# An H3 convolution block with an MLP on one core: SyncE's transfers wait for the landing of the sixth ahead in place of the fourth

## The chip, the cores and the metric

The kernel runs on one core of a Trainium2 chip. The core has a matrix engine (TensorE, PE in the profile; its weight loads are PEld), a vector engine (VectorE, DVE), a scalar engine (ScalarE, ACT), a general engine (GpSimd, POOL) and a fifth one, SyncE (SP), which here does nothing but issue transfers between the chip's memory (HBM) and the core's own buffer (SBUF). Sixteen DMA engines carry these transfers. The metric is the device time of one execution in microseconds. Three executions of the kernel before took 695.85, 694.62 and 696.65 us; their median, 695.85 us, is the time before.

## The reference

With S = 2048 positions, D = 640 channels and F = 1728 hidden features, all in float32:

```python
x = A_q
mod = (_silu(c) @ w_mod).reshape(c.shape[0], 6, 1, -1)
sa, ca, ga, sb, cb, gb = (mod[:, 0], mod[:, 1], mod[:, 2], mod[:, 3], mod[:, 4], mod[:, 5])
h = _layernorm(x, axis=-1) * (1 + ca) + sa
x = x + ga * _A_ref(h, A_k, A_v, A_shift_k, A_ssm_k, A_ssm_D)
h = _layernorm(x, axis=-1) * (1 + cb) + sb
x = x + gb * _B_ref(h, B_w1, B_b1, B_w2, B_b2)
return x
```

`_A_ref(q, k, v, ...)` convolves k with 4 taps per channel, multiplies by v (the product is called kv), convolves kv along the whole sequence with a kernel of 2048 taps per channel (written as an FFT of length 4096, a product and the inverse), adds `kv * ssm_D`, and multiplies by q. `_B_ref` is a matmul with w1, a bias, a squared relu, a matmul with w2 and a bias.

## The kernel before, in words

**The two halves.** The first half, up to some 290 us, is the convolution block. It runs over five blocks b of 128 channels. The long convolution is an FFT built of matmuls: `unit_a` (L383, the first factor: small matmuls of 64 columns, tile `pa`), `spectrum` (L398, tiles `x`, `h` and `eh`), a product on DVE and POOL, `back` (L464, tile `qp`), `unit_t` (transposes, L530) and `unit_y` (L541, tile `y`). `unit_a` for block b + 1 is spread over the second part of block b. The second half is the MLP: eight chunks of 256 positions by fourteen blocks of 128 hidden features, with `mlp_front` (L720, tile `h`) and `mlp_back` (L790, tile `acc`). Its weights and the intermediate result x1 come in by DMA.

**The transfers.** Nearly every transfer is issued by SyncE through one helper, `sp_dma` (L138). In the first half these are, block by block: k and v for the short convolution (tile `KV`, 256 KB each); the kernel ssm_k, in four parts (tile `p`, rows of 256 bytes); kv, stored to a scratch tensor `kv_d` and loaded back transposed in four parts (also into `p`); q whole (`q`, for the layernorm's statistics) and by channel block (`xp`); tables (`gb`, `gi`); slices of w_mod (`wm`, 320 KB each), from which the rows of the modulation are summed on ACT and POOL and taken up by PE (`mr`); and stores of x1 (`x_d`). SyncE runs its instructions in order, so a transfer that waits holds back all that are written behind it. ACT issues eight small transfers and POOL two, on queues of their own.

**What sets the order.** The order of the work in the first half is written out by hand in a table: `at(GS(1, 5), ...)` puts calls at a numbered place between the units of block 1. At the end of the program `keep_order` ties each engine's instructions to the order in which they were written. A transfer's place in SyncE's order is therefore fixed. Three things can hold it there: its data or its buffer (semaphores of PE, DVE, ACT, POOL), the landing of an earlier transfer on which it depends, and the rule in `sp_dma`: once more than `OUT` transfers have been issued, each waits for the landing of the one that stands `OUT` places ahead of it:

```python
def sp_dma(o, i):
    sp.dma_start(o, i)
    queued.append(nc.cur_bb.bb.instructions[-1].name)
    if len(queued) > OUT:
        info = mybir.DependencyInfo(mybir.DependencyClass.Sync, mybir.DependencyReason.DATA)
        tc.add_manual_dep(nc.cur_bb.bb.instructions[-1], queued[-1 - OUT], info, reason="place in time")
```

With `OUT = 4` (L29) no more than four of SyncE's transfers are under way at a time. Landings are told through eight semaphores, which SyncE's and ACT's transfers use in turn.

Of the kernel before, what the change touches and what calls it, by code (L numbers as in the profile page):

```python
# [25 lines left out]
NC = S // CH  # L26
EPS = 1e-5
MLAG = 3
OUT = 4  # L29


def _constants():
# [60 lines left out]
def ssm_mlp_kernel(  # L93
# [43 lines left out]
# [7 lines that stand above are left out]
# [1135 lines left out]
```

## Time and profile before

| what | us |
|---|---|
| median of three executions | 695.85 |
| the profiled execution's own time | 693.38 |
| its span, first to last instruction | 691.6 |
| PE busy in the span | 657.0 |
| DVE, ACT, POOL busy | 335.9, 330.1, 311.4 |

The granted TensorE clock of the profiled execution was 0.997 on the mean. SyncE issued 243 transfers; the core's DMA engines moved 74.76 MB, at 108 GB/s over the span.

How to read it: "busy" is time in which an engine executes; waiting, branching and the issue of transfers do not count. The page cuts the span into 40 slices and gives a digit for each, in tenths of full. A row such as "A L1 <- B x L2: 6.1, 6, 2.0" in the view of waits says that engine A, at line 1, was idle for 6.1 us in total, 6 times and 2.0 us at the longest, until B at line 2 released it; "issue" in place of B means that nothing which the profile shows released it. The chain of waits follows the work that ended last back to the start, each piece with its start and its duration. In the view of windows each engine has its busy time and, in brackets, its number of instructions; behind these stand the granted clock, the share of the sixteen DMA engines and GB/s. Rows of DMA queues give packets, megabytes and the share of the stretch; q1 is SyncE's queue, and queues of the kind "instruction" carry the engines' instructions. Rows of DMA issues give the count, the size of each and the median time from issue to landing.

### The profile page before, as it was taken

To read this page: it belongs to the slowest core of one execution; us is meant where nothing else is said; L and a number is where in the kernel's file an instruction comes from. 1 tells how busy PE (TensorE), PEld (TensorE's weight loads), DVE (VectorE), ACT (ScalarE), POOL (GpSimd) and SP (SyncE) were. 2 spreads that over 40 slices of the span, in tenths; PEclk is the share of its full clock that TensorE was granted. 3 is DMA by queue.
4 is the path that set the end of the run, shared out by engine and by line. 5 is a ranking of instruction groups with operands and counts; after the bars stand their busy time and mean duration, and the time that the engine had idled before them with its cause. 6 is when DMAs were issued, how large, how long until landed. Compare 5 with 4: busy or idle time off the path is not lost.

```text
span 691.6 us, 21100 instructions
## 1 busy us (share of the span) xinstructions
PE 657.0 (95%) x9164; PEld 630.8 (91%) x9164; DVE 335.9 (49%) x601; ACT 330.1 (48%) x688; POOL 311.4 (45%) x390
## 2 busy tenths in 40 slices
PE   6699898889999999999999999999999999999996
PEld 4689798778898888889999999999999999999996
DVE  5267584658886697487532322323332332422313
ACT  4436656767976976466324333333233233233221
POOL 1062165359869789443523514415325325225213
PEclk9999999999999999999999999999999999999999
DMA  9897998889671643466020010100200200200101
GB/s 234 244 270 230 233 265 233 236 204 233 191 221 34 173 148 113 127 199 181 1 77 1 26 52 1 41 37 1 77 1 1 77 1 1 77 1 1 39 1 39
DMA packets 110960, 74.76 MB, mean 108 GB/s; under 512 B 48658, under 2 KB 96146, under 8 KB 110868
## 3 DMA queue, kind: packets, MB, share of 16 engines
q1 hardware_dynamic: 108912, 72.87, 37.2%
q8 instruction: 72, 1.18, 0.7%
q10 hardware_dynamic: 1892, 0.54, 0.4%
q14 instruction: 20, 0.16, 0.1%
q0 software_dynamic: 64, 0.01, 0.0%
HBM read 58.98 MB, written 14.42 MB: 106 GB/s over the span
## 4 chain that ended last, share of the span: by engine, by line
PE 81%; DVE 6%; ACT 5%; DMA 4%; issue 2%; POOL 1%; DVEq 0%; POOLq 0%; ACTq 0%; SPq 0%
PE acc L790 27%; PE h L720 26%; PE qp L464 5%; PE pa L383 4%; PE x L398 4%; PE y L541 4%; PE h L398 3%; DMA wm<-in_w_mod_dram 3%; PE t L530 2%; PE h L711 1%; PE xtp L685 1%; DVE KV L261 1%; ACT wx L146 1%; DVE kacc L261 1%; PE vt L276 1%
## 5 line engine op out<-in xcount | busy, mean ns | idle before, releaser
L151 POOL TENSOR_TENSOR mtmp<-mtmp 128x256 f32<-128x256 f32 x112 | 71.4, 638 | 244.4 <-ACT mtmp L752 236.5
L720 PE MATMUL h<-xt,w_S 128*128 128x256 f32 x1290 | 167.5, 281 | 1.1 <-DVE w_S L157 1.1
L720 PEld LDWEIGHTS h<-xt,w_S 128*128 128x128 f32 x1290 | 161.7, 190 | 1.3 <-DVE w_S L157 1.3
L790 PE MATMUL acc<-w_S,hring 128*128 128x320 f32 x960 | 156.6, 311 | 0.2 <-DVE hring L157 0.2
L157 DVE TENSOR_TENSOR hring<-mtmp,hring 128x256 fp32r<-128x256 f32 x112 | 65.4, 584 | 168.3 <-ACT hring L146 168.3
L790 PEld LDWEIGHTS acc<-w_S,hring 128*128 128x128 f32 x960 | 141.7, 188 | 0.8 <-DVE hring L157 0.7
L752 ACT ACTIVATE mtmp<-h,b1t 128x256 f32<-128x256 f32 x104 | 49.4, 475 | 174.0 <-PE h L720 170.8
L146 ACT ACTIVATE hring<-mtmp 128x256 fp32r<-128x256 f32 x112 | 46.5, 416 | 48.8 <-POOL mtmp L151 47.5
L383 PE MATMUL pa<-wx,p 64*64 64x64 f32 x2560 | 49.3, 228 | 10.8 <-issue 6.1
L383 PEld LDWEIGHTS pa<-wx,p 64*64 64x64 f32 x2560 | 43.9, 141 | 16.8 <-issue 11.3
L146 ACT ACTIVATE a<-pa 128x512 f32<-128x512 f32 x80 | 43.5, 608 | 19.7 <-PE pa L383 19.2
L151 DVE TENSOR_TENSOR wx<-x,wx 128x512 f32<-128x512 f32 x64 | 40.8, 683 | 18.9 <-PE x L398 7.7
L541 PE MATMUL y<-wx,wx 128*64 128x64 f32 x1280 | 43.9, 224 | 2.9 <-ACT wx L146 1.6
L541 PEld LDWEIGHTS y<-wx,wx 128*64 128x64 f32 x1280 | 39.9, 138 | 7.4 <-issue 3.4
L398 PE MATMUL x<-a,gb 128*64 128x128 f32 x640 | 41.6, 274 | 3.3 <-DVE wx L151 2.1
L687 DVE TENSOR_SCALAR we<-xtp,cbs 128x256 f32<-128x256 f32 x35 | 19.0, 543 | 46.8 <-PE xtp L685 46.8
L398 PEld LDWEIGHTS x<-a,gb 128*64 128x64 f32 x640 | 35.9, 137 | 4.9 <-PE h L398 3.0
L154 POOL TENSOR_TENSOR wm<-wm,wm 128x640 f32<-128x640 f32 x20 | 32.1, 1606 | 16.9 <-ACT wm L341 16.5
L261 DVE SCALAR_TENSOR_TENSOR KV<-kt,tap,KV 128x511 f32<-128x511 f32 (+2 forms) x48 | 35.9, 748 | 7.6 <-ACT ktail L146 6.0
L146 ACT ACTIVATE q<-qp 128x512 f32<-128x512 f32 (+1 forms) x40 | 21.3, 584 | 35.4 <-PE qp L464 35.4
L398 PE MATMUL h<-a,gb 128*64 128x128 f32 x512 | 34.0, 275 | 1.5 <-ACT wx L146 1.5
L790 PE MATMUL acc<-w_WX,hring 128*128 128x320 f32 x192 | 31.4, 312 | 0.0
(142 smaller groups left out, 1014.2 us busy)
## 6 DMA issues: line engine op xcount, KB each, us to landing
wm<-in_w_mod_dram SPq DMA_DIRECT2D x25, 320.0 KB, 4.1
KV<-in_A_k_dram SPq DMA_DIRECT2D x20, 256.0 KB, 4.6
KV<-in_A_v_dram SPq DMA_DIRECT2D x20, 256.0 KB, 4.4
p<-in_A_ssm_k_dram SPq DMA_DIRECT2D x20, 256.0 KB, 4.7
p<-kv_d SPq DMA_DIRECT2D x20, 256.0 KB, 4.1
xp<-in_A_q_dram SPq DMA_DIRECT2D x20, 256.0 KB, 4.3
q<-in_A_q_dram SPq DMA_DIRECT2D x15, 320.0 KB, 4.5
out_dram<-x SPq DMA_DIRECT2D x14, 320.0 KB, 2.2
```

Source lines behind the costliest of these rows:

```text
L146: act.activation(o, i, AF.Copy)
L151: eng.tensor_mul(o, a, b)
L154: eng.tensor_add(o, a, b)
L157: eng.tensor_sub(o, a, b)
L261: dve.scalar_tensor_tensor(o, tk[:, : 512 - t], tap[:, b, t : t + 1], o, op0=ALU.mult, op1=ALU.add)
L383: pe.matmul(t[e][64 * r : 64 * r + 64, g].rearrange("p m d -> p (m d)"), pt[b][l, i, 8 * q + g, :], cw[l, r], start=True, stop=True,)
L398: pe.matmul(t[64 * a : 64 * a + 64, s + r], gb[:, g, r, a], AX[b][i][:, 2 * g + a], start=True, stop=True,)
L464: pe.matmul(t[a][:, u], gi[l, 4 * j + u, r], w[r][l, u % 2], start=(r == 0), stop=(r == 1),)
L541: pe.matmul(y[64 * h : 64 * h + 64, 4 * (g % 2) + i].rearrange("p c l d -> p (c l d)"), tss[g][:, i, 64 * r : 64 * r + 64], ca[:, r, h], s ...
L720: pe.matmul(hps[n, f][:m], WI[1, f][:, a, b], XT[n][:, x, b], start=(b == 0 and i == 0), stop=(b == NB - 1 and i == 2),)
L752: act.activation(r[:m], h[:m], AF.Relu, bias=b1t[:m, f : f + 1])
L790: pe.matmul(acc[2 * s + i], h[:, a, s * P : (s + 1) * P], w[:, y, i * 320 : (i + 1) * 320], start=(f == 0 and ti == 0), stop=(f == NF - 1 ...
```

## The change

The constant `OUT` goes from 4 to 6. Each of SyncE's transfers, from the seventh on, then waits for the landing of the sixth ahead of it, and no more than six are under way. Nothing else differs: the instructions on PE, DVE, ACT and POOL are the same in the same order, and SyncE's transfers too; on SyncE only the semaphores that are waited for differ.

```diff
 NC = S // CH
 EPS = 1e-5
 MLAG = 3
-OUT = 4
+OUT = 6
```

## The prediction

> **What bounds the kernel now.** I read the page first, then the windows by stage, what PE and SP wait for, the chain of waits, and last the DMA queues of single stretches.
>
> ```profile
> span 691.6 us, 21100 instructions
> PE 657.0 (95%) x9164; PEld 630.8 (91%) x9164; DVE 335.9 (49%) x601; ACT 330.1 (48%) x688; POOL 311.4 (45%) x390
> DMA  9897998889671643466020010100200200200101
> ...
> q8 instruction: 72, 1.18, 0.7%
> ```
>
> PE is idle for 691.6 - 657.0 = 34.6 us. The DMA engines are nearly full for the first third and almost empty after it. The windows say where the idle time lies:
>
> ```profile
> core 0: us, PE busy (x) PEld busy (x) DVE busy (x) ACT busy (x) POOL busy (x), PEclk, DMA share, GB/s
> 60.00:90.00 30.00, 26.58 (x765) 24.24 (x758) 20.53 (x43) 18.84 (x36) 5.69 (x17) 1.00 0.91 252
> ...
> 120.00:150.00 30.00, 25.26 (x632) 22.30 (x634) 18.68 (x40) 19.58 (x36) 11.89 (x16) 1.00 0.75 213
> ...
> 205.00:240.00 35.00, 33.28 (x894) 30.20 (x892) 22.08 (x32) 27.99 (x58) 28.45 (x27) 1.00 0.34 95
> ...
> 320.00:680.00 360.00, 360.00 (x2756) 360.00 (x2755) 116.73 (x234) 120.87 (x270) 128.06 (x160) 1.00 0.08 28
> ```
>
> From 320 us on PE never stops, so nothing done to transfers can move that half: whatever the change is worth is decided before. There PE loses 3.4 us (60 to 90) and 4.7 us (120 to 150) where the DMA engines are full, and 1.7 us of 35 where they are a third full, with more matmuls in it (894). What PE waits for, longest first:
>
> ```profile
> PE pa L383 <- issue: 6.1, 6, 2.0
> PE kt L239 <- DMA KV<-in_A_k_dram: 4.3, 1, 4.3
> PE pa L383 <- DMA p<-kv_d: 3.1, 2, 2.3
> ```
>
> The largest row is "issue": no semaphore holds PE. And on the chain of waits:
>
> ```profile
> 21.47 3.14 DMA kv_d<-kacc
> ...
> 27.71 5.22 PE pa L383 x214
> 32.93 1.58 issue
> 34.51 0.83 PE pa L383 x39
> ...
> 79.50 0.61 issue
> ...
> 82.99 1.36 issue
> ...
> 114.65 0.40 issue
> ...
> 120.35 4.30 DMA wm<-in_w_mod_dram
> ...
> 124.73 6.76 DMA wm<-in_w_mod_dram
> ...
> 140.88 7.30 DMA wm<-in_w_mod_dram
> ```
>
> Four of these issue stalls (1.58, 0.61, 1.36, 0.40 us) are on it, all in the middle of a run of the 64-column pa matmuls. My reading is that PE's next instructions have not arrived. Queue q8 carries 72 packets, and PE has 2 x 9164 = 18,328 matmuls and weight loads: one packet for each 255, so a fetch for each 127 matmuls. A pa run takes 5.22 us for 214, some 3.1 us for 127: faster than anywhere else. The DMA queues of the stretch 31.9 to 32.4 us have one such packet, just before PE stops at 32.93; those of 310 to 680 us have 23, and PE waits for none of them:
>
> ```profile
> q8 instruction: 1, 0.02, 13.9%
> ```
> ```profile
> q8 instruction: 23, 0.38, 0.4%
> ```
>
> So a fetch that meets full DMA engines is late, and one that meets empty ones is not.
>
> **The change, part by part.** No instruction is added or moved; the order on all five engines is the same. Only SP's waits change: transfer n waits for the landing of n-6, not n-4. Waits for data stay. What SP waits for in 0 to 175 us (first and last of the thirteen DMA rows over 0.1 us, and the largest other row):
>
> ```profile
> SPq L138 <- DMA wm<-in_w_mod_dram: 12.6, 11, 3.8
> ...
> SPq L138 <- PE mr L323: 3.6, 3, 2.1
> ...
> SPq L138 <- DMA tap<-in_A_shift_k_dram: 0.2, 1, 0.2
> ```
>
> The thirteen rows sum to 80.9 us, all others to some 18: for 82% of SP's waiting the change lets it go on, until it stands six deep or meets a wait for data.
>
> *Do transfers land sooner?* Time to landing, in this full stretch and where a transfer is nearly alone:
>
> ```profile
> q1 hardware_dynamic: 69112, 40.82, 86.8%
> ...
> KV<-in_A_k_dram SPq DMA_DIRECT2D x18, 256.0 KB, 4.6
> ```
> ```profile
> out_dram<-x SPq DMA_DIRECT2D x14, 320.0 KB, 2.2
> ```
> ```profile
> x_d<-xp SPq DMA_DIRECT2D x15, 256.0 KB, 2.6
> ```
>
> With three ahead it is 4.6 us, alone 2.2 to 2.6: each transfer ahead costs about (4.6 - 2.4) / 3 = 0.7 us. The 40.82 MB in 175 us on q1 are 233 GB/s, about what four transfers of 256 KB in 4.6 us make (228). Four lone transfers in 2.4 us would be 437 GB/s, so the path is full, not the count of four. With six I expect 4.6 + 2 x 0.7 = 6.0 us to landing at the same rate, and transfers that land when they did. Two places on the chain can gain. The store at 21.47 took 3.14 us, alone 2.6: with the gb loads ahead of it issued earlier, 0 to 0.5; I take 0.3. The wm transfer at 124.73 goes out as that of 120.35 lands (124.65), the fourth ahead of it; SP was ready after its issue at 123.36 (0.46 us), so 0 to 0.8; it stands in the same line, so I take 0.4. Gain: 0.7 us.
>
> ```profile
> 123.36 0.46 SPq L138 DMA_DIRECT2D kv_d<-KV  x1
> ```
>
> *What is later?* Everything that shares the DMA engines and isn't SP's own, and that is the fetches. If a fetch waits for what stands in the engines ahead of it, two more transfers delay it by 2 x 0.7 = 1.4 us, and as PE is already standing when it comes, the stall grows by as much. If it doesn't wait for them, 0. The row of 310 to 680 us, with no stall, against 6.1 us of them in the full part is nearer to the first. At 34.51 and 115.05 four p loads went out just before:
>
> ```profile
> 24.68 2.92 SPq L138 DMA_DIRECT2D p<-kv_d  x4
> ...
> 115.30 4.74 SPq L138 DMA_DIRECT2D p<-kv_d  x4
> ```
>
> Their issue held SP for 2.92 and 4.74 us (the issue above took 0.46), so there SP gets perhaps one further ahead, 0.7 us. The four stalls on the chain then cost 2 x 1.4 + 2 x 0.7 = 4.2 us; times the 82%, 3.4. A fifth adds nothing, as the chain runs over the wm loads beside it:
>
> ```profile
> 131.39 0.45 PE L383 MATMUL pa<-wx,p 64*64 64x64 f32 x13 [2.01 <-issue]
> ```
>
> Fetches that now come just in time may start to stall; how near they are no row shows, so 0 to about 2 us (as many stalls again at half the price), and I take 0. No later stage gives any of it back: it is PE's time, and PE is the bound.
>
> Sum: 3.4 - 0.7 = +2.7 us on this execution, whose own time is 693.38 (span 691.6, 1.78 around it): 696.1. It lies 2.47 below the median of the runs, 695.85, so the median goes to 698.6 (698.55).
>
> [...]
>
> **The rivals.**
> (1) The fetch is not held by SP's line. The stalls stay, the gains stand: -0.7 us, 695.2. For it: the stalls differ by a factor of four (0.40 to 1.58 us) with the same four transfers in flight. Against it: no issue stall after 310.
> (2) More in flight fills the engines better, on the other side. In 0 to 175 us the rate is 233 GB/s; from 60 to 90 it is 252. If the whole part went at 252, the three wm loads on the chain (18.4 us) lose 8%, 1.4 us, and with the two gains at their upper ends (0.5 + 0.8) that is 2.7; shorter waits between them may bring it to 4: 692 to 693.2. It decides if the fetches aren't late. Against it: the time to landing already contains 2 us of standing in line, so the engines have work.
> (3) SP can't go further ahead at all: its issues are held (2.92 and 4.74 us for four) and data waits come first. Then nothing changes, 695.85. Against it: the 80.9 us.
> (4) The delay reaches fetches that don't stall now: +3.4 + 2 and the fifth stall: about +6, 702.
>
> **How the numbers follow.** Forecast 0.50, rival (1) 0.23, (2) 0.13, (3) 0.06, (4) 0.08. The measurement can tell about 0.3%, 2.1 us. The forecast's bounds are half of the stalls' growth with the whole gain, 0.5 x 4.2 - 0.7 = +1.4, and four stalls at 1.4 with no gain, +5.6; some three quarters of it lies over +2.1. Slower: 0.37 + 0.08 = 0.45; faster: (2), 0.13; within 0.3%: the rest, 0.42. The range leaves out most of (2) and what lies over (4): 694.0 to 702.0; the forecast's own is 697.3 to 701.5.
>
> **What would show it.** Right: the median time to landing of the k, v and p loads goes from 4.6 to about 6; the mean rate before 175 us stays near 233 GB/s; the PE row "pa <- issue" grows from 6.1 us to 10 or more, the stalls at the places of 32.93, 79.5 and 82.99 by 0.7 to 1.4 each; after 320 us PE runs as before. Wrong: landing times of 6 us with an unchanged issue row (rival 1); a rate near 252 and shorter wm pieces on the chain (2); landing times that stay at 4.6 (3). I would also be wrong if SP's place in line pushed some data load of PE's later, which the rows "PE <- DMA" would show.

## The result, and the profile after

The changed kernel took 700.22 us (median of nine executions) where the kernel before took 695.80 in the same session: a ratio of 1.0073, 95% interval 1.0044 to 1.0103; 4.4 us by the medians and 5.1 by the ratio. Run again in a later session, as one of the experiments below (`after2`), it took 697.27 against 694.82: 1.0039, 1.0014 to 1.0065, 2.5 to 2.7 us. So it is slower, by 0.4 to 0.7%. The forecast was +2.7 us. The medians are of all executions; the ratios, here and below, leave out those over 1.5% above the fastest of the same kernel (one of `after`, one of `after2`, two of `late6b`).

The profiled execution took 698.78 us. Its page, and its windows at the places shown of before:

```profile
span 697.0 us, 21099 instructions
...
PE 661.8 (95%) x9164; PEld 636.7 (91%) x9164; DVE 335.4 (48%) x601; ACT 329.8 (47%) x688; POOL 311.5 (45%) x390
```
```profile
60.00:90.00 30.00, 27.82 (x832) 25.17 (x831) 21.85 (x46) 20.26 (x39) 6.15 (x16) 1.00 0.79 227
120.00:150.00 30.00, 29.66 (x818) 26.56 (x809) 22.58 (x46) 25.09 (x46) 16.03 (x22) 1.00 0.83 235
205.00:240.00 35.00, 31.36 (x821) 28.46 (x819) 23.73 (x31) 26.69 (x55) 29.96 (x30) 1.00 0.36 100
320.00:680.00 360.00, 360.00 (x2756) 360.00 (x2755) 118.96 (x239) 123.24 (x274) 126.46 (x158) 1.00 0.09 32
```

PE is idle for 697.0 - 661.8 = 35.2 us, 0.6 more than before, though the span is 5.4 longer: the same 9164 matmuls also took 4.8 us more (the clock, below). From 320 us on PE never stops, as before. The window that stands out is 120 to 150: PE loses 0.3 us there, where it lost 4.7 before. What PE waits for, longest first:

```profile
PE pa L383 <- issue: 5.3, 5, 2.3
PE y L541 <- issue: 5.2, 3, 3.2
PE pa L383 <- DMA p<-kv_d: 4.8, 1, 4.8
PE kt L239 <- DMA KV<-in_A_k_dram: 4.2, 1, 4.2
```

and, in the same view of before, the second row of "issue":

```profile
PE y L541 <- issue: 1.0, 1, 1.0
```

The stalls for "issue" went from 7.1 (6.1 and 1.0) to 10.5 us: the expected sign and nearly the expected size. But the row that was to grow to 10 or more, that of pa, fell from 6.1 to 5.3. Of the four stalls that were to grow, one did, from 1.58 us at 32.93 to 2.29 at 36.19; that of 1.36 at 82.99 is 0.95 at 89.99, and those at 79.50 and 114.65 are gone. The chain of waits:

```profile
22.88 4.25 DMA kv_d<-kacc
...
36.19 2.29 issue
...
40.59 3.68 PE x L398 x32
...
47.00 1.90 PE x L398 x32
...
89.99 0.95 issue
...
115.41 1.99 PE qp L464 x29
...
165.70 1.27 PE mr L323 x4
...
183.32 0.70 issue
...
188.70 0.99 issue
...
194.65 0.34 issue
...
236.50 3.18 issue
```

and, in the chain of before, the same two places of PE's work and PE's longest stall for issue after 165 us:

```profile
108.84 1.99 PE qp L464 x29
...
166.24 1.27 PE mr L323 x4
...
234.76 0.99 issue
```

PE reaches the qp run 6.6 us later than before (115.41 against 108.84) and the mr matmuls 0.5 us earlier (165.70 against 166.24). The three wm loads, 18.4 us of the chain of before, are no longer on it: PE came late enough not to wait. So all that was lost up to 115 us was made up by 166, and the 5.4 us by which the span grew were lost after it: 5.2 us stand in four stalls, three of them where before had none over 0.2 us, and the clock (below) adds to them.

The transfers and their rate, in 0 to 175 us:

```profile
q1 hardware_dynamic: 69098, 40.82, 86.3%
...
KV<-in_A_k_dram SPq DMA_DIRECT2D x18, 256.0 KB, 5.4
```

Landing, of the k loads, went from 4.6 to 5.4 us, and SP's queue moved the same 40.82 MB. What SP waits for there is mostly no longer landings: their rows sum to 15.9 us in place of 80.9. The two longest:

```profile
SPq L138 <- POOL wm L154: 12.6, 6, 3.3
SPq L138 <- PE vt L276: 11.7, 5, 7.8
```

### The profile page after: what moved, and what is told of

The parts are those of the page before. It is cut to its first block, busy times and chain, and to the rows that moved or that the text cites. A ratio compares the mean times of both kernels' runs of the same rounds, so it can differ in the third digit from the quotient of the medians.

```text
span 697.0 us, 21099 instructions
## 1 busy us (share of the span) xinstructions
PE 661.8 (95%) x9164; PEld 636.7 (91%) x9164; DVE 335.4 (48%) x601; ACT 329.8 (47%) x688; POOL 311.5 (45%) x390
## 4 chain that ended last, share of the span: by engine, by line
PE 85%; DVE 5%; DMA 3%; ACT 3%; issue 2%; POOL 1%; DVEq 0%; POOLq 0%; ACTq 0%; SPq 0%
PE acc L790 27%; PE h L720 26%; PE x L398 5%; PE pa L383 5%; PE qp L464 5%; PE y L541 5%; PE h L398 4%; PE t L530 2%; PE h L711 1%; DVE KV L261 1%; PE xtp L685 1%; PE kt L239 1%; PE vt L276 1%; DMA kv_d<-KV 1%; PE gr L928 1%
## 5 line engine op out<-in xcount | busy, mean ns | idle before, releaser
L383 PE MATMUL pa<-wx,p 64*64 64x64 f32 x2560 | 51.6, 235 | 12.5 <-issue 5.3
L383 PEld LDWEIGHTS pa<-wx,p 64*64 64x64 f32 x2560 | 46.1, 148 | 18.7 <-issue 13.9
L398 PE MATMUL x<-a,gb 128*64 128x128 f32 x640 | 43.1, 281 | 2.5 <-DVE wx L151 1.5
L398 PEld LDWEIGHTS x<-a,gb 128*64 128x64 f32 x640 | 37.5, 141 | 3.7 <-PE h L398 1.9
L157 POOL TENSOR_TENSOR we<-wx 128x256 f32<-128x256 f32 x20 | 16.1, 807 | 36.1 <-DVE wx L151 36.1
```

The lines of the kernel that those rows point to most:

```text
L157: eng.tensor_sub(o, a, b)
L383: pe.matmul(t[e][64 * r : 64 * r + 64, g].rearrange("p m d -> p (m d)"), pt[b][l, i, 8 * q + g, :], cw[l, r], start=True, stop=True,)
L398: pe.matmul(t[64 * a : 64 * a + 64, s + r], gb[:, g, r, a], AX[b][i][:, 2 * g + a], start=True, stop=True,)
```

## The experiments

Two theories were put to the test. **S**: the line of transfers sets PE's time near 150 us, so PE's lateness before it is swallowed. **F**: more transfers in flight hold PE's instruction fetches back, and after some 165 us nothing swallows it. Their rivals: **G**: six in flight shortened the wm loads (a real gain that made up for a real loss), and **C**: the late stalls fall as they may.

In all of them but `after2` the depth becomes a function of the transfer's number n in SyncE's order (n = 38 is issued near 48 us, 139 near 177, 163 near 210):

```diff
-OUT = 4
+OUT = lambda n: 6 if n < 38 else 4
...
-        if len(queued) > OUT:
+        if len(queued) > (ahead := OUT(len(queued) - 1)):
...
-            tc.add_manual_dep(nc.cur_bb.bb.instructions[-1], queued[-1 - OUT], info, reason="place in time")
+            tc.add_manual_dep(nc.cur_bb.bb.instructions[-1], queued[-1 - ahead], info, reason="place in time")
```

This table has all of them. The three columns of places say how much later than in the profile of before PE starts the same matmul: the first of the qp run that before starts at 109 us, the first mr at 166, and the first gr (L928) at 287. The two columns of stalls are the rows "PE <- issue" summed, in the view of waits up to 165 us and from 165 to 300. Places and stalls come from one profiled execution each, the ratio from 8 to 12 executions (6 for `late2` and `all3`) against 9 to 35 of before. `front6`, `mid6`, `late6` and `all8` share theirs of before (median 693.85 us), so do `six4`, `late3`, `late2` and `all3` (693.94), and `after2`, `late6a`, `late6b` and `tail2` (694.82).

| kernel | ahead | at 109 | at 166 | at 287 | stalls to 165 | stalls after | ratio to before, interval |
|---|---|---|---|---|---|---|---|
| before | 4 | 0 | 0 | 0 | 6.3 | 1.2 | |
| late6b | 4; 6 from 163 on | +0.2 | -3.1 | +1.1 | 5.0 | 4.1 | 0.9965, 0.9931 to 1.0000 |
| tail2 | 4; 2 for 163 to 172 | +5.5 | +3.8 | +6.0 | 6.7 | 1.0 | 0.9995, 0.9967 to 1.0022 |
| late6a | 4; 6 for 139 to 162 | +4.3 | -0.6 | +0.4 | 7.1 | 1.9 | 1.0016, 0.9994 to 1.0038 |
| late6 | 4; 6 from 139 on | +2.1 | -0.6 | +3.6 | 5.7 | 4.4 | 1.0028, 0.9995 to 1.0061 |
| late3 | 4; 3 from 139 on | +4.3 | -0.6 | +5.0 | 3.9 | 1.4 | 1.0052, 1.0032 to 1.0072 |
| late2 | 4; 2 from 139 on | +5.0 | +0.6 | +13.4 | 4.9 | 0.4 | 1.0204, 1.0171 to 1.0238 |
| front6 | 6 up to 37; 4 | +4.2 | -2.6 | +0.6 | 6.6 | 2.6 | 1.0040, 1.0013 to 1.0067 |
| mid6 | 4; 6 for 38 to 138; 4 | +6.8 | +0.6 | +1.3 | 7.4 | 1.4 | 1.0010, 0.9983 to 1.0036 |
| six4 | 6 up to 138; 4 | +5.4 | -1.8 | -0.1 | 7.4 | 2.4 | 1.0003, 0.9980 to 1.0026 |
| after | 6 | +6.6 | -0.5 | +5.4 | 5.2 | 5.2 | 1.0073, 1.0044 to 1.0103 |
| after2 | 6 | +6.6 | +0.2 | +2.4 | 8.8 | 2.9 | 1.0039, 1.0014 to 1.0065 |
| all8 | 8 | +9.0 | +1.0 | +4.7 | 7.9 | 3.5 | 1.0038, 1.0003 to 1.0074 |
| all3 | 3 | +6.6 | +7.8 | +10.4 | 2.3 | 1.3 | 1.0196, 1.0169 to 1.0223 |

**One part of the change at a time.**

`front6`:

> Six ahead for transfers 0 to 37 only (up to some 48 us), four for all later ones. Theory S (the line of transfers sets PE's time near 150 us, so PE's lateness before it is swallowed): PE is 5 to 7 us behind the kernel before from 40 to 110 us, within 1 us of it at 155 us, and the median is within 1 us of before. Rival G (the wm loads of 120 to 150 us were shortened by the two more transfers in flight, and without these the front's loss stays): the wm loads stay on the chain with some 18 us, PE is still 5 to 7 us behind at 155 us, and the median is 5 to 7 us over before.

`mid6`, with `6 if 38 <= n < 139 else 4`:

> Six ahead for transfers 38 to 138 only (48 to 175 us), four before and after. Theory S: PE keeps the times of before up to 48 us and comes to 155 us within 1 us of before; the median is within 1 us of before. Rival G: the wm loads on the chain shrink as they did in the changed kernel, PE is 5 to 7 us ahead at 155 us, and the median is 5 to 7 us under before.

`late6`, with `6 if n >= 139 else 4`:

> Six ahead for transfers 139 and later only (from some 177 us on), four before. Theory F (two more transfers in flight hold PE's instruction fetches back, and after 155 us nothing swallows it): stalls of 0.3 to 1.0 us each at 183, 189 and 195 us and one of some 3 us near 236 us, 5 us behind from 242 us on, median 4 to 6 us over before: the whole loss of the changed kernel. Rival C (the late stalls hang on how the fetches happened to fall, PE having come 6 us late through the front): no new stall over 0.3 us, median within 1 us of before.

In all three traces PE is within 2.6 us of before at 166, however late it was at 109 (4.2, 6.8, 2.1), if not within the 1 us that S expected. In `front6` PE makes up 6.8 us between 109 and 166, and the wm loads leave the chain, although only four transfers were in flight there: G isn't needed for it. `mid6` is nowhere ahead of before by 5 to 7 us, as G had it. `late6` shows F's stalls (4.4 us after 165), though as three of 1.4 to 1.6 us and not with one of some 3 near 236. Its ratio of 1.0028, some 2 us, has an interval that just takes in 1 and lies under the 4 to 6 expected. `front6` came out 2.7 us over before by its median where S expects nothing. That was not expected and stays open: its own trace has +0.6 us.

`six4`, the changed kernel with its last part undone (`6 if n < 139 else 4`):

> Six ahead for transfers 0 to 138 (up to some 175 us), four for all later ones: the changed kernel without its last part. Theories S and F: PE is 4 to 8 us behind before at 100 us and within 2.6 us of it at 165 us, as in the runs so far; the issue stalls after 165 us sum to 1 to 3 us, not to 5.2 as in the changed kernel; the median is within 2 us of before. Rival G (what the first half loses stays): 4 us or more over before, as the changed kernel.

This is the plainest of the runs: the time is that of before (1.0003), though at 109 us PE is 5.4 us late. Its waits after 165 us, and those of `after` and `late2` from the same view:

```profile
PE pa L383 <- issue: 1.4, 2, 1.2
PE y L541 <- issue: 1.0, 1, 1.0
```
```profile
PE y L541 <- issue: 3.2, 1, 3.2
PE pa L383 <- issue: 2.0, 3, 1.0
```
```profile
PE pa L383 <- issue: 0.2, 1, 0.2
PE y L541 <- issue: 0.2, 1, 0.2
```

**More and fewer.**

`all8`, with 8 throughout:

> Eight ahead for all transfers. Theories S and F together: PE further behind at 40 to 110 us than with six (8 us or more), again within 1 us of before at 155 us, then issue stalls longer than with six, the row of y and pa waiting for issue 12 us or more in all, median 702 to 707 us. Rival: with six ahead SP is already held by its data waits and not by landings, so eight changes nothing more: median 699 to 701 us. If the fetches are not held by the line, the issue rows stay at 10 us.

PE is 9.0 us late at 109 and 1.0 at 166, and the issue rows sum to 11.4 us; but the time, 697.75 us, lies under the 702 to 707 expected and no further from its own before (1.0038) than six does, as its rival has it. By then SP is held by other things; its largest wait in 0 to 175 us is for a wm buffer:

```profile
SPq L138 <- POOL wm L154: 21.4, 7, 9.3
```

`all3`, with 3 throughout:

> Three ahead for all transfers. By the landing times (2.4 us alone, 0.7 us for each transfer ahead) three take 3.8 us and move 207 GB/s at most, against 233 with four: theory S (the line sets the time near 150 us) then has PE some 10 to 18 us behind before at 165 us, and a median 9 to 17 us over before, although the issue rows of pa and y fall from 7 to under 4 us. If PE's own work and the fetches set the time there, PE is 2 to 6 us ahead of before instead, and the median under it.

The window of 0 to 175 us and the landing of k:

```profile
0.00:175.00 175.00, 149.14 (x3372) 133.90 (x3372) 100.26 (x190) 96.72 (x185) 69.25 (x117) 0.96 0.81 224
```
```profile
KV<-in_A_k_dram SPq DMA_DIRECT2D x18, 256.0 KB, 4.1
```

The last number of the window is GB/s: 224, where the same view gives 237 with four, 237 with six and 236 with eight. At 224 the swallowing is gone: PE is 6.6 us late at 109 and 7.8 at 166, and the median is 12.9 us over before, within the 9 to 17 expected; the 7.8 us are somewhat under the 10 to 18 expected. That fits S: the rate bounds PE's time at 166, and four in flight already give all of it. The issue rows fell to 3.6 us in all, as F expects, and it didn't help.

`late3` and `late2`, with 3 and 2 from transfer 139 on:

> Three ahead for transfers 139 and later, four before. Theory F: the issue stalls after 165 us sum to under 1 us (1.2 in the kernel before, 1.4 and 2.6 in two others with four ahead there); median 0 to 2 us under before. Rival C (the stalls fall as they may, whatever stands in the line): they sum to 1 to 5 us, median within 2 us of before on either side.

> Two ahead for transfers 139 and later, four before. Theory F: issue stalls after 165 us of 0.5 us or less in all; if no data comes late, the median is 1 to 3 us under before. If two no longer feed PE in time, rows of PE waiting for DMA or for mr, t or y behind a late load appear after 177 us, and the median is 1 us or more over before. Rival C: stalls as with four.

With two the stalls went to 0.4 us, as F expects; with three they are 1.4, over the 1 us expected and within the 1.2 to 2.6 of four throughout. The times did not fall, since data came late. The chain of `late3`:

```profile
179.51 4.56 DMA kv_d<-KV
...
184.14 4.07 DMA x_d<-xp
...
188.27 4.87 DMA kv_d<-KV
...
193.25 0.04 ACT KV L241
```

and PE's longest wait in it after 165 us (5.5 us in `late2`):

```profile
PE mc L350 <- ACT wx L146: 2.6, 1, 2.6
```

A store of kv has to land before SP lets a store of x1 go, whose landing lets the next store of kv go, and ACT, which is to fill the KV buffer again, waits for that one to land. With four in flight none of the three is on the chain of before. So fewer isn't the better kernel either.

**Which of the late transfers.**

> The changed kernel once more, six ahead throughout, beside the next three on one chip. Theories S and F: PE within 2.6 us of before at 165 us however late it is at 100 us; issue stalls after 165 us of 3.5 to 6 us in all (5.2, 4.4 and 3.5 in the three runs with six or eight ahead there), where four ahead gave 1.2 to 2.6; median 3 to 6 us over before. Rival C: stalls after 165 us anywhere from 1 to 5 us.

> Six ahead for transfers 139 to 162 only (some 177 to 203 us), four elsewhere. Theory F: the stalls between 180 and 200 us sum to 1.5 to 3 us (2.0 in the changed kernel, 3.0 and 2.5 in the two others with six or eight; 0.2 to 1.6 with four), that near 236 us stays at 0.7 to 1.0 us; median 1 to 3 us over before.

> Six ahead for transfers 163 and later only (from some 210 us on), four before. Theory F: stalls between 180 and 200 us as with four (0.2 to 1.6 us), that near 236 us 1.0 to 3.2 us (3.2 in the changed kernel, 1.4 and 1.0 in the two others); median 0 to 3 us over before.

> Two ahead for transfers 163 to 172 only (some 210 to 236 us, the last before the stall near 236 us), four elsewhere. Theory F: that stall, 0.7 to 1.0 us with four, goes to 0.4 us or less (0.4 with two, 0.7 with three ahead in the earlier runs), and everything else stays: the median is 0 to 1 us under before. Rival: the x and weight loads come too late, PE waits for them after 240 us, and the median is over before.

`late6a` is `6 if 139 <= n < 163 else 4`, `late6b` is `6 if n >= 163 else 4`, `tail2` is `2 if 163 <= n < 173 else 4`. `after2` came out under what was expected of it: 2.9 us of stalls after 165 us for 3.5 to 6, and 2.5 us over before for 3 to 6. `late6a` lies under its 1 to 3 us too by its medians (695.20 against 694.82). The stall of y near 236 us is the cleanest dose: with two ahead in 163 to 172 it is 0.2 us (`late2`) or absent (`tail2`), with three 0.7 and 0.7, with four 1.0, 1.0, 1.0, 1.0 and 0.7, with six 3.2, 1.4, 1.3 and 1.3; with eight 1.0 again. Between 180 and 200 us it isn't clean: `late6b` has 2.8 us there with four ahead, `late6a` 0.9 with six. C has its share: which fetch meets how full a line differs from run to run by as much as the depth adds. `late6b` came out under before (0.9965, up to 1.0000; by the medians 694.12 against 694.82 us, 0.9990), against the expectation and within what the measurement can tell from no change; its own trace has +1.1 us, so no claim of a faster version rests on it. `tail2` lost its stall, with no gain that can be seen.

That the stall near 236 us is a late fetch is seen in the DMA queues. In `after`, from 232 us to just before PE stops at 236.50, this is the only queue with packets:

```profile
q1 hardware_dynamic: 1970, 0.99, 82.6%
```

and from 236.4 to 238.6 us the instruction queue has its packet:

```profile
q1 hardware_dynamic: 464, 0.46, 62.6%
q8 instruction: 1, 0.02, 2.7%
```

In the kernel before the packet stands in 231 to 234.7 us, ahead of the stall at 234.76, which then took 0.99 us:

```profile
q1 hardware_dynamic: 1732, 0.95, 89.9%
q8 instruction: 1, 0.02, 1.7%
```

PE was 1.7 us behind before at this place. In `after` the fetch began after PE had run out (the packet at 237.39, the stall at 236.50), in `before` ahead of it (233.33 and 234.76). The issues of the 10 us from 225 to 235, in `after`:

```profile
xp<-in_A_q_dram SPq DMA_DIRECT2D x4, 256.0 KB, 3.3
...
w1s<-in_B_w_dram SPq DMA_DIRECT2D x1, 320.0 KB, 7.4
w2s<-in_B_w_dram SPq DMA_DIRECT2D x1, 320.0 KB, 7.6
```

The two weight loads took 4.9 us each before: with six allowed they joined a line that four would have kept shorter. When the fetch was asked for, no view shows.

The traces' records of the instruction queue say more, as PE's 9164 matmuls are the same in the same order in all fourteen. Between 20 and 300 us PE stops for issue 93 times in these traces, at twelve places of its program only, which lie multiples of some 127 matmuls apart: one fetch's worth. Each stop ends 1.0 to 1.7 us after the packet of a fetch has ended. So "issue" is here PE waiting for its instructions.

The fetch ahead of the stall near 236 us begins when PE has started 5065 matmuls in `late2`, with two in flight, 5122 in `before`, and 5163, where PE stands, in `after`. Take for each fetch the earliest such place in any of the traces, and count from when PE is there until the fetch begins. For the 39 fetches from 24 to some 242 us this delay is 0.74 us on the mean with three in flight (`all3`), 0.93 with four (`before`), 1.10 and 1.14 with six (`after`, `after2`) and 1.20 with eight (`all8`). For the first six of them, up to some 62 us, it is 0.6 to 1.2 us in the eight traces with four there, 1.4 to 1.7 in the four with six, and 1.7 with eight. The packet itself takes the same in the full part and in the quiet one, 1.1 us on the mean in `before`. So what more transfers in flight lengthen is the time until the fetch begins; what holds it there, the traces don't show.

## Why the prediction was right, and where its steps were wrong

**Right: the fetches.** That fetches which meet a longer line are late, that PE stands for it, and that the whole is a few us, held. Rival (1), that the stalls stay as they are, would have left the issue rows at 7.1 us and the time at 695.2. The delays of the fetches speak against it, as they grow with the number of transfers in flight: 0.74 us on the mean with three, 0.93 with four, 1.10 and 1.14 with six, 1.20 with eight. Where the DMA engines are nearly empty (a share of 0.08 in `before` and 0.09 in `after` from 320 to 680 us) PE waits for none of its fetches: from 310 to 680 us q8 has 23 packets in `before` and 22 in `after`, and there is no stall for issue in either. Up to 240 us it waits for some, as the 7.1 and 10.5 us of issue stalls show.

**Wrong: where they count.** The step that failed is "The four stalls on the chain then cost 2 x 1.4 + 2 x 0.7 = 4.2 us; times the 82%, 3.4", for those at 32.93, 79.5, 82.99 and 114.65, with "No later stage gives any of it back". The next pieces of the same chain were the three wm loads, 18.4 us, and the prediction used them to price the fifth stall at nothing, but not the four ahead of it. Yet all five stand ahead of waits that PE has there anyway: it can come some 4 to 7 us later to the wm loads and be through at the same time. The seven kernels that share the program of before up to transfer 138 (the first seven rows of the table) reach 109 us at 0 to 5.5 us after its profile, 3.0 on the mean, and 166 us at -0.1 on the mean; the four with six in flight between (`mid6`, `six4`, `after`, `after2`) 6.3 and -0.4. So the change costs 3.3 us up to 109 us, about the forecast's size, and nothing of it is left at 166. Up to the mark at 109 us the four lose 3.1 us more in stalls for issue than the seven; their matmuls take 2.1 us longer, in more stretches at half the clock (last section); and their other waits are 1.9 us shorter. Nor do the four stalls carry it alone: that at 32.93 is 0.6 to 2.5 us long in the eight traces with four there and 2.3 to 3.3 in the four with six, and that at 114.65 is in no trace but `before`.

Three readings behind the price were wrong as well. The row of p loads at 115.30 begins after the stall had ended at 115.05, and four other transfers went out between the p loads of 24.68 and the stall at 32.93, so the half price at these two places had no ground. The 5.22 us of 214 pa matmuls lie partly at half the clock (28.02 to 31.43 us); elsewhere 64 take 1.09 us, so 127 take some 2.2 and not 3.1. And a fetch begins 0.5 us later with six in flight than with four in the first 62 us and 0.2 us later over all, not 1.4.

**Wrong: what was put at nothing.** "Fetches that now come just in time may start to stall", of which the prediction said "0 to about 2 us" and "I take 0". They did at once: at a place that PE reaches at 70 to 76 us the four traces with six in flight there have a new stall of 1.7 to 2.2 us, `all8` one of 1.4, and the nine others none. It is swallowed with the rest. The stalls after 165 us carry the loss: 1.2, 2.6, 1.4 and 2.4 us with four throughout that part (`before`, `front6`, `mid6`, `six4`; 1.9 on the mean), 5.2, 2.9 and 4.4 with six (`after`, `after2`, `late6`; 4.2). From 166 to 287 us the former lose 1.4 us on the mean against the profile of before, the latter 4.1: +2.7 us, with single values from 0 to 3.2 and from 2.3 to 6.0. Of the 2.7 us, 2.3 are stalls and 0.9 slower matmuls, less 0.5 of other waits. That the sum agrees with the forecast is luck: one term went to nothing and another took its place.

**The gains.** That at the kv_d store did not come: on the chain it took 4.25 us in place of 3.14. That at the wm loads, 0.4 us, can't be told from the waits that a late PE no longer has. With four in flight and a lateness of 4.2 to 5.5 us at 109 (`front6`, `late6a`, `late3`, `late2`, `tail2`), PE makes up 6.8, 4.9, 4.9, 4.4 and 1.7 us by 166, 4.5 on the mean; the four with six there make up 6.2 to 7.1, 6.7 on the mean. So G may hold for some 2 us of it, and S is too strong as it was put: the transfers bound PE's time at 166 from below, and a late PE is through when its own work is.

**Landing.** Forecast 6.0 us, measured 5.4 and, in `after2`, 5.2: a rise of 0.6 to 0.8 us rather than 1.4. SP's waits for landings fell from 80.9 to 15.9 us, so it is soon held by its data and buffers instead.

**The other rivals.** (2), fuller engines: 237 GB/s with four and six, so no. (3), SP can't go further: it could, as the landings show, but it explains why eight does no more than six. (4), more fetches come to stall: they do, at 70 to 76 us and after 165 us, though not on top of the rest.

**What the first comparison of two traces suggested, and was not so.** PE's 6.6 us at 109 us looked like the start-up's doing in `after` (a later d load, a later store). The repeats show that half of it is the spread between executions of one program. `front6`, with the same first 38 transfers, is 4.2 us late there, and `tail2`, with those of before, 5.5. What stays open: `front6`'s median, and how much of the 0.4 to 0.7% lies in the mean of the stalls, which three or four traces on each side with overlapping values cannot say. The parts' medians do not add to better than some 2 us.

## What to carry to other kernels

A stall on the chain is worth its time only if no later stage is paced by something else: look down the same chain for long DMA pieces before adding stalls up, and take those behind the last such stage first. Allow as many transfers in flight as fill the DMA engines and no more; here four did (237 GB/s, as with six), and six only made the landing longer, 5.4 us for 4.6, and the instruction fetches later (a delay of 1.10 and 1.14 us on the mean, for 0.93). Kernels that agree up to a point are repeats of one another up to it, and show what a difference between two traces is worth.

## What was not expected of the hardware

A stall of the matrix engine can cost more than its own length. After the stall of 3.18 us in `after` the windows show the granted clock, third from the end:

```profile
239.70:240.40 0.70, 0.70 (x24) 0.70 (x26) 0.00 (x0) 0.02 (x1) 0.57 (x1) 1.00 0.99 252
240.40:243.80 3.40, 3.40 (x83) 2.95 (x77) 0.00 (x0) 0.60 (x1) 0.00 (x0) 0.50 0.65 105
243.80:250.00 6.20, 6.20 (x182) 5.81 (x176) 4.66 (x6) 5.77 (x12) 3.92 (x3) 1.00 0.35 100
```

3.40 us at half the clock do 1.7 us of work, so 1.7 us are lost on top. With it the last part of `after` adds up: 4.0 us more of stalls and 1.7 of clock, 5.7, against 6.0 measured between the marks at 166 and 287. The same is seen in the chain after the wait and the stall near 36 us: 32 x matmuls take 3.68 us at 40.59 and 1.90 at 47.00. Not every stall does it: that of 1.40 us at 237.95 in `late6` left the clock at 1.00. The traces' records of the clock have the length of this stretch throughout: up to 300 us there are 45 stretches at half the clock in all fourteen, each 3.41 us long or two or three times that, and within a trace they begin multiples of 3.41 us apart (at 28.78, 39.02 and 240.41 us in `after`, for 6.83, 6.83 and 3.41 us). PE was not wholly idle ahead of them: 40 of the 45 follow 3.41 us in which PE was busy for 6 to 50% of the time, the other five 58 to 87%; for the stretches named here and that at 28.02 in `before` it is 12, 33, 21 and 32%. Ahead of the stretch at 240.41 PE was idle for 2.7 us of the 3.41 and ran for the last 0.7 at the full clock. What halves the clock, the traces don't show.

The half-clock stretches are a good part of what sets two executions apart: counted in units of 3.41 us, `before` has one up to 109 us, the other six with four in flight throughout that part one to three, the four with six in flight from 48 us on three or four.
